# Mamba-2 scan into a SwiGLU layer: mean of squares by four 32-column tiles, the roots spread by a load, and a new order of steps

## The chip, the cores and the metric

The kernel runs on one core of a Trainium2 chip. The core has five engines that run side by side, each through its own list of instructions in order: TensorE (PE; its weight loads are shown apart as PEld), VectorE (DVE), ScalarE (ACT), GpSimd (POOL) and SyncE (SP). SP here only issues transfers (DMAs), which 16 DMA engines carry out; ACT issues four at the start. Matrix products read operands from SBUF and write into banks of PSUM, from where DVE or ACT take them. The metric is device time of one execution in microseconds.

## The reference, cut to what matters

```python
# part one: batch, heads, seq, head_dim, d_state = 4, 8, 768, 32, 16
log_a = np.log(np.clip(a, 1e-6, 1.0))
for c in range(nc):                       # chunks of 32 along seq
    cum = np.cumsum(la, axis=-1)
    L = np.exp(cum[:, :, :, None] - cum[:, :, None, :]) * causal
    y_intra = (einsum('bhin,bhjn->bhij', Cc, Bc) * L) @ xc
    y_inter = einsum('bhin,bhnd->bhid', Cc, state) * np.exp(cum)[..., None]
    y[:, :, sl] = y_intra + y_inter
    state = decay_full * state + sum over j of Bx * decay_from_j
# part two: 3072 tokens, d_model 256, d_ff 1536
rms = np.sqrt(np.mean(x * x, axis=-1, keepdims=True) + 1e-06)
xn = x / rms * rms_g
g = xn @ w_gate
val = xn @ w_val
out = (g / (1 + np.exp(-g)) * val) @ w_out
```

Everything is float32. `x` of part two is y with the heads side by side: one row of 256 values for each of 3072 tokens. `rms` is one number for each token; the change is about how it is computed and handed to the 128 partitions.

## The kernel before, in words

The 3072 tokens are worked in six blocks of 512, each made of two pairs of 256 tokens (pair = two chunks of 128, cut in halves of 64 from the third pair on). Activations lie transposed: a partition is a feature, a column a token. Part one gives, for a block, y in PSUM (the steps `turn`, `T`, `Tt`, `Td`: transposes of B and C and their copies; `g`, `gg`, `L`, `L1`: products and decays; `A`, `S`: state additions and states; `y`: outputs). Then, for each block:

- `sq` (L733 to L749): ACT squares y, POOL adds the two halves of the 256 features, so `sqs[blk]` is 128 partitions by 512 tokens. `yt` copies y to SBUF.
- `ms` (`norm_sums`, L772): one product on PE with the constant `mean` (128 x 128, all 1/256) as weights and `sqs[blk]` as the moving operand. All 128 output partitions hold the same 512 means.
- `rs` (`norm_roots`, L776 and L777): ACT takes Ln and then Exp with scale -0.5, which is one over the root, on 128 x 512 into `r`.
- `xn` (`norm_apply`, L784): DVE multiplies y, the gains and `r`, one half of the features at a time. Block 0 has another form (L788), and its first two weight products run ahead of the roots (`early`, `norm`).
- `tx` (L868): differences of the quarters of xn. Gate and value products then follow Winograd's form of Strassen's scheme: seven products instead of eight, `P.k.j` for k of 1 to 7 and j of 0 to 5 (L891). `take` (L897) copies a bank to SBUF on ACT, `C` (L903) adds on DVE, `silu` (L912) runs on ACT, `hid` (L916) multiplies on DVE. Block 0 uses plain products (`gate`, L807) for its first six columns of weights and `P` for the others.
- `O.k.j` (L981) is the projection to the output by the same scheme; block 0 has the plain `o` (L923). `Otake`, `Oadd` and `out` end it.

Weights come in eight-byte words and are cut down to float32 while the first block runs: `fetch` loads a piece (k of 0 to 19), `pow` (ACT, L182 to L185), `man` and `wt` (DVE, L192 to L201) convert it; `cw` and `two` make sums of weights. `bc.p` and `x.p` load B, C and x of a pair, `rowout` and `rowe` store rows of decays to DRAM, and `dT` and `spread` load them back spread over partitions (L530, L461). `bank` takes a PSUM bank out of two that these steps share.

The order of work is written out by hand: the string `order` names some 1,540 steps, `block:step.numbers/slot`, and they are issued in exactly this order. Each engine, and SP as the queue of transfers, executes its part of that list in order, and semaphores hold an instruction until what it reads is there and what it overwrites is read. From block 1 on, a step written under block n that belongs to part one or to the norm (`ms`, `rs`, `xn`, `y` and others) works for block n+1; `1:ms` is for block 2. Tiles of one tag share buffers: `r` has the tag `sq2` (one buffer), row tiles have `r_sb` (three). A step that needs exponentials after a SiLU, or the other way, makes ACT load a table; `table` and `exps` load one ahead of need.

Of the kernel before, what the change touches and what calls it, by code (L numbers as in the profile page):

```python
# [9 lines left out]
FP32 = mybir.dt.float32  # L10
# [10 lines left out]
def kernel(  # L21
# [35 lines left out]
    P = 128  # L57
# [709 lines left out]
    xns = {}  # L767

    def norm_sums(blk):

        ps["m", blk] = ms = bank("ms", (P, TB))
        nc.tensor.matmul(out=ms, lhsT=mean, rhs=sqs[blk], start=True, stop=True)  # L772

    def norm_roots(blk):
        ps["r", blk] = r = nrm.tile([P, TB], FP32, tag="sq2", name="r", bufs=1)
        nc.scalar.activation(out=r, in_=ps.pop(("m", blk)), func=AF.Ln, bias=eps)  # L776
        nc.scalar.activation(out=r, in_=r, func=AF.Exp, scale=-0.5)  # L777

# [312 lines left out]
    def by_vector(out, in_, scale):  # L1091
# [25 lines left out]
        "ms": norm_sums, "rs": norm_roots, "xn": norm_apply,  # L1117
# [27 lines left out]
    def of_chunk(n, fn):  # L1145
# [19 lines left out]
        "ms": when(1, norm_sums), "rs": when(1, norm_roots), "xn": when(1, norm_apply),  # L1165
# [7 lines left out]
        0:warm 0:a 0:set 0:bc.0 0:bc.1 0:x.0 0:x.1 0:ident 0:fetch.0 0:ones 0:zeros 0:fetch.1 0:upto  # L1173
        0:gcol 0:never 0:after 0:fetch.2 0:mid 0:ident16 0:whole16 0:fetch.3 0:idle.7 0:mask.0.0/1
        0:mask.0.1/0 0:hmask 0:part 0:part2 0:fetch.4 0:head 0:mids 0:fetch.5 0:bc.2 0:x.2 0:fetch.6
        0:aT 0:la0 0:log4.0.4 0:fetch.7 0:log 0:fetch.9 0:mask.1.1/2 0:log4.4.2 0:log4.6.2 0:sel
        0:upto2 0:after2 0:whole 0:r.0 0:tmask 0:fetch.15 0:parts.0 0:middles 0:c*2 0:turn.0.1
        0:T.0.1 0:cx 0:kinks 0:eps 0:Tt.0.0.1 0:d 0:dx 0:Tt.0.1.1 0:sums.0.1 0:exp.0.1 0:turn.0.0
        0:Tt.0.0.0 0:T.0.0 0:Tt.0.1.0 0:scale.1 0:cc 0:sums.0.0 0:exp.0.0 0:scale.0 0:mean
        0:turn.1.0 0:never16 0:g.0.1/0 0:L.0.1 0:man.0 0:turn.1.1 0:T.1.1 0:Tt.1.1.0 0:Tt.1.1.1  # L1180
        0:Tt.1.0.0 0:T.1.0 0:Tt.1.0.1 0:sums.1.1 0:exp.1.1 0:g.0.0/1 0:L.0.0 0:bc.4 0:man.1 0:pow.0
        0:last.0 0:Tl.0 0:A.0 0:S.0 0:pow.1 0:mask.1.0/0 0:sums.1.0 0:exp.1.0 0:wt.0 0:g.1.1/2
        0:L.1.1 0:pow.5 0:row.1 0:rowout.1 0:rowe.1 0:wt.1 0:g.1.0/1 0:L.1.0 0:man.5 0:fetch.8
        0:last.1 0:Tl.1 0:man.2 0:y.0/0 0:mask.3/2 0:A.1 0:S.1 0:wt.5 0:r.1 0:y.1/1 0:sq.0 0:yt.0
# [185 lines left out]
```

## Time and profile before

| | |
|---|---|
| time, three runs | 408.11, 407.00, 405.97 us; median 407.0 |
| the profiled execution | 407.43 us, of which the span of instructions is 405.7 |
| granted PE clock in it | 0.999 of full |
| busy: PE, DVE, ACT, POOL | 398.3, 300.1, 220.9, 36.6 us |
| matmul passes | 3851 |
| DMA | 25.35 MB, mean 62 GB/s |
| ACT table loads | 16, 1283 ns each |

Times of the profile count from the start of the span. A line of the timeline gives start, length, engine, line of the kernel, operation, what is written from what, the shape and how many instructions were merged; in brackets the engine's idle time before them and what ended it. `128*32` is the part of the PE array that a pass uses, rows by columns. A float32 matmul appears as two passes. Matmuls overlap in a pipeline and their ends are modelled, so a group's cost is read from its start to the start of the next one. A PE that counts as busy can still be waiting inside.

### The profile page before, as it was taken

To read this page: it belongs to the slowest core of one execution; us is meant where nothing else is said; L and a number is where in the kernel's file an instruction comes from. 1 tells how busy PE (TensorE), PEld (TensorE's weight loads), DVE (VectorE), ACT (ScalarE), POOL (GpSimd) and SP (SyncE) were. 2 spreads that over 40 slices of the span, in tenths; PEclk is the share of its full clock that TensorE was granted. 3 is DMA by queue.
4 is the path that set the end of the run, shared out by engine and by line. 5 is a ranking of instruction groups with operands and counts; after the bars stand their busy time and mean duration, and the time that the engine had idled before them with its cause. 6 is when DMAs were issued, how large, how long until landed. Compare 5 with 4: busy or idle time off the path is not lost.

```text
span 405.7 us, 9479 instructions
## 1 busy us (share of the span) xinstructions
PE 398.3 (98%) x3851; PEld 340.1 (84%) x3851; DVE 300.1 (74%) x686; ACT 220.9 (54%) x451; POOL 36.6 (9%) x57
## 2 busy tenths in 40 slices
PE   8999999999999999999999999999999999999997
PEld 4556467888888899888899988899988899988896
DVE  5998999979877878468799348788358676266682
ACT  3899796975756334655554545360754462544500
POOL 4010010002300011300023000010500010000000
PEclk9999999999999999999999999999999999999999
DMA  9897997800001041550350000330100000100001
GB/s 112 229 253 165 216 227 129 175 18 0 2 1 53 11 135 42 66 75 29 82 93 2 13 0 2 90 109 2 52 2 0 2 4 0 53 0 2 0 2 53
DMA packets 88995, 25.35 MB, mean 62 GB/s; under 512 B 76888, under 2 KB 82776, under 8 KB 88952
## 3 DMA queue, kind: packets, MB, share of 16 engines
q1 hardware_dynamic: 84792, 24.49, 27.8%
q10 hardware_dynamic: 4160, 0.26, 0.7%
q8 instruction: 30, 0.49, 0.5%
q14 instruction: 13, 0.11, 0.1%
HBM read 21.33 MB, written 3.41 MB: 61 GB/s over the span
## 4 chain that ended last, share of the span: by engine, by line
PE 84%; SPq 4%; DVE 4%; DMA 4%; ACT 2%; issue 1%; ACTq 0%; DVEq 0%
PE gate L891 28%; PE o L981 23%; PE val L891 21%; PE o L923 5%; PE y L699 3%; SPq L121 2%; SPq L128 1%; PE g L562 1%; DMA wr<-in_moe_w_gate_dram 1%; DMA dT<-rowe 1%; PE ms L772 1%; PE tp L505 1%; DMA br<-in_B_dram 1%; SPq L160 1%; DVE h L840 1%; DMA rowe<-e_sb 1%
## 5 line engine op out<-in xcount | busy, mean ns | idle before, releaser
L903 DVE TENSOR_TENSOR c<-val,p 128x512 f32<-128x512 f32 x99 | 67.4, 687 | 40.8 <-PE val L891 32.6
L897 ACT COPY p<-gate 128x512 f32<-128x512 f32 x99 | 57.5, 584 | 55.9 <-PE gate L891 54.3
L891 PE MATMUL gate<-tx,sw 128*128 128x256 f32 x264 | 66.1, 381 | 0.0
L912 ACT ACTIVATE c<-c 128x256 f32<-128x256 f32 x99 | 39.6, 417 | 41.6 <-DVE c L903 41.4
L891 PEld LDWEIGHTS gate<-tx,sw 128*128 128x128 f32 x264 | 49.3, 190 | 7.8 <-ACT p L897 1.0
L916 DVE TENSOR_TENSOR h<-c 128x256 f32<-128x256 f32 x99 | 40.1, 418 | 16.1 <-ACT c L912 16.0
L891 PE MATMUL val<-xn,sw 128*128 128x256 f32 x132 | 33.7, 380 | 0.0
L891 PE MATMUL val<-tx,sw 128*128 128x256 f32 x132 | 33.6, 381 | 0.0
L891 PE MATMUL gate<-xn,wgv 128*128 128x256 f32 x132 | 33.4, 383 | 0.0
L891 PE MATMUL val<-xn,wgv 128*128 128x256 f32 x132 | 33.4, 379 | 0.0
L891 PE MATMUL gate<-tx,wgv 128*128 128x256 f32 x132 | 33.2, 380 | 0.0
L475 POOL TENSOR_SCALAR_AFFINE_SELECT L<-L 64x512 f32<-64x512 f32 x32 | 23.0, 719 | 79.1 <-ACT L L473 77.6
L981 PE MATMUL o<-wo,h 128*128 128x128 f32 x240 | 30.1, 276 | 0.0
L981 PEld LDWEIGHTS o<-wo,h 128*128 128x128 f32 x240 | 28.9, 192 | 1.4 <-issue 0.7
L981 PE MATMUL o<-two,h 128*128 128x128 f32 x240 | 29.1, 275 | 0.0
L981 PEld LDWEIGHTS o<-two,h 128*128 128x128 f32 x240 | 28.2, 192 | 1.0 <-issue 0.7
L981 PE MATMUL o<-two,s 128*128 128x128 f32 x240 | 28.7, 275 | 0.0
L997 ACT COPY v<-o 128x256 f32<-128x256 f32 x15 | 5.7, 377 | 41.9 <-PE o L981 41.9
L981 PEld LDWEIGHTS o<-two,s 128*128 128x128 f32 x240 | 27.8, 192 | 0.1
L891 PEld LDWEIGHTS val<-tx,sw 128*128 128x128 f32 x132 | 24.8, 190 | 3.5 <-issue 0.2
L891 PEld LDWEIGHTS gate<-tx,wgv 128*128 128x128 f32 x132 | 24.8, 190 | 3.4
L891 PEld LDWEIGHTS val<-xn,sw 128*128 128x128 f32 x132 | 24.8, 190 | 3.3
(184 smaller groups left out, 636.5 us busy)
## 6 DMA issues: line engine op xcount, KB each, us to landing
L<-rowd SPq DMA_DIRECT2D x32, 128.0 KB, 3.5
xr<-in_x_dram SPq DMA_DIRECT2D x24, 128.0 KB, 3.1
wr<-in_moe_w_out_dram SPq DMA_DIRECT2D x6, 512.0 KB, 6.1
wr<-in_moe_w_gate_dram SPq DMA_DIRECT2D x5, 512.0 KB, 4.5
wr<-in_moe_w_val_dram SPq DMA_DIRECT2D x5, 512.0 KB, 7.3
out_dram<-ob SPq DMA_DIRECT2D x9, 256.0 KB, 2.4
br<-in_B_dram SPq DMA_DIRECT2D x22, 64.0 KB, 4.0
cr<-in_C_dram SPq DMA_DIRECT2D x22, 64.0 KB, 2.6
```

The lines of the kernel that those rows point to most:

```text
L121: queues[i].dma_start(out=dst[:, i], in_=src[b, :, sl, :].rearrange("h s n -> s h n"))
L128: queue.dma_start(out=st[p]["x"][:, i], in_=x[b, :, sl, :].rearrange("h s n -> s h n"))
L475: nc.gpsimd.affine_select(out=L[r], in_=L[r], pattern=[[0, NH], [1, HC]], compare_op=ALU.is_ge, fill=0.0, base=0, channel_multiplier=-1)
L699: nc.tensor.matmul(out=y[2 * k + u][rows, (2 * n + i) * HC:(2 * n + i + 1) * HC], start=(k, u, rows.start) not in opened, stop=True, skip_ ...
L891: nc.tensor.matmul(out=dst[:, half[w]], lhsT=lhsT, rhs=rhs, start=(k in (1, 2, 5) and w == 0), stop=True, skip_group_check=True)
L897: nc.scalar.copy(out=t, in_=Xs[j])
L903: nc.vector.tensor_tensor(out=t, in0=Zs[j], in1=a, op=ALU.add)
L912: nc.scalar.activation(out=u, in_=src[:, half[0]], func=AF.Silu)
L916: nc.vector.tensor_tensor(out=hidden_tile(blk, j)[:, c // 10 - 1, c % 10 - 1], in0=u, in1=src[:, half[1]], op=ALU.mult)
L923: nc.tensor.matmul(out=o, lhsT=hs_[blk, f // 2][:, f % 2, k // 2, (k % 2) * P:(k % 2 + 1) * P], rhs=wo[:, f], start=opens, stop=(f == NF - ...
L981: nc.tensor.matmul(out=o[t] if apart else o[:, t * P:(t + 1) * P], lhsT=lhsT[:, t], rhs=rhs, start=(k in (1, 2, 4, 5) and j == 0 and (apar ...
L997: nc.scalar.copy(out=ts[k], in_=halves_of(Os["X"]))
```

## The change

For blocks 1 to 5 the one `ms` product is replaced by four: `mean` is cut to 32 columns, and each product takes 128 of the 512 tokens and writes 32 partitions of a 128 x 128 result (`tile_position` names the 32 columns of the array). Partition 32k+q then holds token 128k+m in column m, 32 times over. Ln and Exp run on 128 x 128. The result is stored to DRAM (`roots`, 64 KB), and a new step `rb` (`spread_roots`) loads one of the 32 equal rows of each group back into all 128 partitions (256 KB into `r`); `xn` is as before. Block 0 keeps its form. The first 12 steps of the order, through `0:fetch.1`, stay; the later ones stand in a new order, with the five `rb` among them. Of the order the diff shows both versions up to block 0's last gate products, and the places around `rs`, `rb` and `xn`.

```diff
--- before.py
+++ after.py
@@ -764,17 +764,35 @@
                  in_=y.rearrange("p u (j m) -> p u j m", j=n))
 
 
-    xns = {}
+    xns, roots = {}, {}
 
     def norm_sums(blk):
 
-        ps["m", blk] = ms = bank("ms", (P, TB))
-        nc.tensor.matmul(out=ms, lhsT=mean, rhs=sqs[blk], start=True, stop=True)
+        if blk == 0:
+            ps["m", blk] = ms = bank("ms", (P, TB))
+            nc.tensor.matmul(out=ms, lhsT=mean, rhs=sqs[blk], start=True, stop=True)
+            return
+        ps["m", blk] = ms = bank("ms", (P, P))
+        for k in range(NT):
+            nc.tensor.matmul(out=ms[32 * k:32 * k + 32], lhsT=mean[:, 0:32],
+                             rhs=sqs[blk][:, k * P:(k + 1) * P], start=True, stop=True,
+                             tile_position=(0, 32 * k), skip_group_check=True)
 
     def norm_roots(blk):
-        ps["r", blk] = r = nrm.tile([P, TB], FP32, tag="sq2", name="r", bufs=1)
+        if blk == 0:
+            ps["r", blk] = r = nrm.tile([P, TB], FP32, tag="sq2", name="r", bufs=1)
+        else:
+            r = nrm.tile([P, P], FP32, tag="r_sb", name="r4", bufs=3)
         nc.scalar.activation(out=r, in_=ps.pop(("m", blk)), func=AF.Ln, bias=eps)
         nc.scalar.activation(out=r, in_=r, func=AF.Exp, scale=-0.5)
+        if blk:
+            roots[blk] = dram.tile([NT, 32, P], FP32, name="roots%d" % blk)
+            nc.sync.dma_start(out=roots[blk].rearrange("t q m -> (t q) m"), in_=r)
+
+    def spread_roots(blk):
+        ps["r", blk] = r = nrm.tile([P, TB], FP32, tag="sq2", name="r", bufs=1)
+        nc.sync.dma_start(out=r.rearrange("p (t m) -> p t m", t=NT),
+                          in_=roots[blk][:, 0].partition_broadcast(P))
 
     def norm_apply(blk):
         r = ps["r", blk]
@@ -1114,7 +1132,7 @@
         "yt": lambda p: taken_out(p, ac.copy),
         "ydone": lambda p: leave(("y", p)),
         "pow": power, "man": mantissa, "wt": weight,
-        "ms": norm_sums, "rs": norm_roots, "xn": norm_apply,
+        "ms": norm_sums, "rs": norm_roots, "rb": spread_roots, "xn": norm_apply,
         "early": lambda f, s: products_early(
             f, s, take("gate", ("gv", f)) if s == 0 else ps["gv", f]),
         "norm": lambda f: (normed(f), leave(("gv", f))),
@@ -1162,7 +1180,8 @@
         "y": of_pair(1, lambda p: outputs(p, pair_of_banks("y", 2) if p % 2 == 0 else None,
                                           [p + 2] if p + 2 < NPAIR else [], p % 2)),
         "sq": when(1, lambda b: squares(2 * b)), "yt": when(1, lambda b: taken_out(2 * b, ac.copy)),
-        "ms": when(1, norm_sums), "rs": when(1, norm_roots), "xn": when(1, norm_apply),
+        "ms": when(1, norm_sums), "rs": when(1, norm_roots),
+        "rb": when(1, spread_roots), "xn": when(1, norm_apply),
         "tx": when(1, combine_x),
         "bc": of_pair(2, load), "x": of_pair(2, load_x), "spread": of_chunk(2, spread), "sub": of_chunk(2, subtract),
         "ex": of_chunk(2, exponential), "scale2": of_pair(2, scale),
@@ -1170,160 +1189,160 @@
         "exps": when(1, lambda b: ac.preload_act_table_set("natural_log_exp_and_others")),
     }
     order = """
-        0:warm 0:a 0:set 0:bc.0 0:bc.1 0:x.0 0:x.1 0:ident 0:fetch.0 0:ones 0:zeros 0:fetch.1 0:upto
-        0:gcol 0:never 0:after 0:fetch.2 0:mid 0:ident16 0:whole16 0:fetch.3 0:idle.7 0:mask.0.0/1
-        0:mask.0.1/0 0:hmask 0:part 0:part2 0:fetch.4 0:head 0:mids 0:fetch.5 0:bc.2 0:x.2 0:fetch.6
-        0:aT 0:la0 0:log4.0.4 0:fetch.7 0:log 0:fetch.9 0:mask.1.1/2 0:log4.4.2 0:log4.6.2 0:sel
-        0:upto2 0:after2 0:whole 0:r.0 0:tmask 0:fetch.15 0:parts.0 0:middles 0:c*2 0:turn.0.1
-        0:T.0.1 0:cx 0:kinks 0:eps 0:Tt.0.0.1 0:d 0:dx 0:Tt.0.1.1 0:sums.0.1 0:exp.0.1 0:turn.0.0
-        0:Tt.0.0.0 0:T.0.0 0:Tt.0.1.0 0:scale.1 0:cc 0:sums.0.0 0:exp.0.0 0:scale.0 0:mean
-        0:turn.1.0 0:never16 0:g.0.1/0 0:L.0.1 0:man.0 0:turn.1.1 0:T.1.1 0:Tt.1.1.0 0:Tt.1.1.1
-        0:Tt.1.0.0 0:T.1.0 0:Tt.1.0.1 0:sums.1.1 0:exp.1.1 0:g.0.0/1 0:L.0.0 0:bc.4 0:man.1 0:pow.0
-        0:last.0 0:Tl.0 0:A.0 0:S.0 0:pow.1 0:mask.1.0/0 0:sums.1.0 0:exp.1.0 0:wt.0 0:g.1.1/2
-        0:L.1.1 0:pow.5 0:row.1 0:rowout.1 0:rowe.1 0:wt.1 0:g.1.0/1 0:L.1.0 0:man.5 0:fetch.8
-        0:last.1 0:Tl.1 0:man.2 0:y.0/0 0:mask.3/2 0:A.1 0:S.1 0:wt.5 0:r.1 0:y.1/1 0:sq.0 0:yt.0
-        0:ydone.0 0:early.0.0/0 0:row.0 0:scale.2 0:pow.3 0:parts.1 0:sums.3 0:man.6 0:pow.2 0:wt.2
-        0:sq.1 0:ms.0 0:yt.1 0:ydone.1 0:early.0.1 0:pow.6 0:fetch.11 0:wt.6 0:rowe.0 0:dT.2 0:man.3
-        0:exp.3 0:rs.0 0:pow.4 0:mask.2/1 0:sums.2 0:exp.2 0:man.7 0:bc.3 0:turn.2 0:T.2 0:wt.3
-        0:early.1.0/2 0:early.1.1 0:Tt.2.1 0:x.4 0:x.3 0:xn.0 0:rowout.0 0:man.4 0:wt.4 0:gate.2/1
-        0:fetch.10 0:norm.0 0:norm.1 0:man.8 0:Tt.2.0 0:Td.2 0:gg.2/0 1:table 0:silu.0 0:hid.0
-        0:pow.7 0:wt.7 0:L1.2.3 0:man.9 0:L.2.0 0:L1.2.2 0:pow.9 0:wt.9 0:silu.2 0:hid.2 0:tx.0
-        0:pow.8 0:wt.8 0:dT.3 0:gate.3/2 0:silu.3 0:hid.3 0:fetch.12 0:pow.11 0:scale.3 0:man.10
-        0:fetch.13 0:A.2 0:S.2 0:gate.4/0 0:silu.4 0:hid.4 0:bc.5 0:fetch.14 0:man.11 0:fetch.16
-        0:cw.3 0:pow.10 0:gate.5/1 0:silu.5 0:hid.5 0:pow.12 0:y.2/2 0:S.3 0:yt.2 0:sq.2 0:ydone.2
...
-        0:o.9 0:hidg.21.5 0:rs.1 0:xn.1 1:P.1.0 1:P.1.1 1:P.2.1 1:P.2.0 0:tx.1 0:ex.11 1:x.0
...
-        1:O.6.5 1:s4.4 1:Otake.6 1:s4.3 2:spread.2 1:spread.3 2:turn.0 2:T.0 2:Tt.0.1 2:Tt.0.0 1:ms
-        1:rs 1:O.7.0 1:O.7.1 1:O.7.2 1:O.7.3 1:O.7.4 1:O.7.5 1:Otake.7 1:O.2.5 1:spread.2 1:sub.2
-        1:sub.0 1:ex.0 1:O.4.5 1:xn 2:P.1.1 2:take.1.1 1:Oadd.22 1:O.3.0 1:O.3.1 1:O.3.2 1:Oadd.11
...
-        2:O.6.3 2:O.6.4 2:O.6.5 2:s4.2 2:s4.1 2:s4.3 1:out.1 2:s4.4 2:rs 3:turn.1 2:xn 2:tx 2:O.2.3
...
-        3:s.5 3:s3.5 3:exps 2:out.1 3:ms 3:rs 3:s.4 3:s3.4 3:O.1.0 3:O.1.1 3:O.1.2 3:O.1.3 3:O.1.4
...
-        4:O.6.3 4:sq 4:ms 4:rs 4:xn 4:s4.2 4:O.2.2 4:O.6.4 4:O.6.5 4:s4.5 4:Otake.6 4:s4.4 4:O.4.1
...
+        0:warm 0:a 0:set 0:bc.0 0:bc.1 0:x.0 0:x.1 0:ident 0:fetch.0 0:ones 0:zeros 0:fetch.1 0:mean
+        0:head 0:upto 0:never 0:after 0:mid 0:upto2 0:gcol 0:mids 0:ident16 0:whole16 0:idle.7
+        0:mask.0.0/1 0:whole 0:hmask 0:tmask 0:part 0:part2 0:sel 0:mask.1.1/0 0:fetch.5 0:after2
+        0:aT 0:la0 0:kinks 0:mask.0.1/2 0:log4.0.4 0:r.0 0:parts.0 0:eps 0:log 0:d 0:dx 0:c*2 0:cx
+        0:log4.4.2 0:log4.6.2 0:scale.0 0:bc.2 0:turn.0.1 0:T.0.1 0:Tt.0.0.1 0:Tt.0.1.1 0:sums.0.1
+        0:exp.0.1 0:turn.0.0 0:Tt.0.1.0 0:T.0.0 0:Tt.0.0.0 0:sums.0.0 0:exp.0.0 0:fetch.2 0:turn.1.1
+        0:T.1.1 0:Tt.1.0.1 0:Tt.1.1.1 0:scale.1 0:cc 0:g.0.1/2 0:L.0.1 0:turn.1.0 0:Tt.1.1.0
+        0:Tt.1.0.0 0:T.1.0 0:sums.1.1 0:exp.1.1 0:A.0 0:S.0 0:A.1 0:S.1 0:man.0 0:g.0.0/1 0:L.0.0
+        0:pow.0 0:wt.0 0:man.5 0:pow.1 0:never16 0:last.1 0:Tl.1 0:mask.1.0/2 0:sums.1.0 0:exp.1.0
+        0:g.1.0/0 0:L.1.0 0:scale.2 0:last.0 0:Tl.0 0:fetch.4 0:fetch.3 0:x.4 0:middles 0:man.1
+        0:g.1.1/1 0:L.1.1 0:fetch.6 0:fetch.7 0:pow.5 0:wt.5 0:y.0/2 0:sq.0 0:pow.3 0:row.1
+        0:rowout.1 0:rowe.1 0:yt.0 0:ydone.0 0:fetch.12 0:y.1/0 0:r.1 0:row.0 0:man.2 0:fetch.9
+        0:fetch.8 0:wt.1 0:early.0.0/1 0:parts.1 0:man.6 0:mask.3/2 0:sums.3 0:pow.2 0:wt.2 0:rowe.0
+        0:rowout.0 0:dT.2 1:dT.0 0:sq.1 0:ms.0 0:yt.1 0:ydone.1 0:early.0.1 0:pow.6 0:wt.6
+        0:fetch.13 0:man.3 0:exp.3 0:rs.0 0:man.7 0:wt.3 0:turn.2 0:pow.4 0:xn.0 0:mask.2/0 0:sums.2
+        0:exp.2 0:early.1.0/2 0:early.1.1 0:man.4 0:wt.4 0:gate.2/0 0:x.2 0:norm.0 0:norm.1 0:T.2
+        0:Tt.2.0 0:Tt.2.1 0:Td.2 0:dT.3 0:gg.2/1 1:table 0:silu.0 0:hid.0 0:gate.3/2 0:tx.0 0:man.8
+        0:pow.7 0:wt.7 0:L1.2.3 0:L1.2.2 0:man.9 0:silu.2 0:hid.2 0:L.2.0 0:pow.9 0:wt.9 0:A.2 0:S.2
+        0:pow.8 0:wt.8 0:silu.3 0:hid.3 0:fetch.11 0:man.11 0:pow.11 0:gate.4/0 0:silu.4 0:hid.4
+        0:bc.3 0:scale.3 0:fetch.10 0:pow.10 0:man.10 0:cw.3 0:gate.5/1 0:silu.5 0:hid.5 0:x.3
...
+        0:rs.1 1:turn.0 0:hidg.11.4 0:hidg.21.4 0:hidg.22.4 1:T.0 1:Tt.0.0 0:silug.21.5 0:hidg.12.4
+        0:P.3.5 0:C.12.5 0:man.19 0:pow.19 0:wt.19 0:hidg.21.5 0:silug.12.5 0:hidg.12.5 0:spread.11
+        0:sub.11 0:ex.11 0:table.0 0:sub.8 0:o.6 0:o.7 0:o.8 0:o.9 0:o.10 1:T.1 1:Tt.1.0 0:rb.1
+        0:xn.1 1:P.1.1 1:take.1.1 1:P.1.0 1:take.1.0 1:P.2.1 1:P.2.0 0:tx.1 1:P.6.1 1:take.6.1
...
+        1:s2.2 1:O.5.3 1:O.5.4 1:s2.4 1:s2.3 1:O.5.5 1:s2.5 1:s3.2 1:s3.0 1:sub.2 1:ms 1:rs 1:O.6.0
+        1:s4.0 1:O.6.1 1:O.6.2 1:s4.1 1:O.6.3 1:O.6.4 1:O.6.5 1:Otake.6 1:s4.3 1:s4.4 2:turn.0 2:T.0
+        2:Tt.0.1 1:rb 1:s4.5 1:s4.2 1:s3.5 2:dT.1 2:turn.1 2:T.1 2:Tt.1.0 2:Tt.1.1 2:Tt.0.0 2:Td.0
...
+        2:scale2.1 1:O.4.3 1:O.4.4 1:O.4.5 1:Oadd.21 1:O.2.3 1:O.2.4 1:O.2.5 1:O.3.0 1:O.3.1 1:xn
+        2:P.1.1 2:take.1.1 2:P.1.0 2:take.1.0 1:tx 1:ex.2 1:spread.1 1:sub.1 1:ex.1 1:O.3.2 1:O.3.3
...
+        2:P.4.5 2:silu.21.5 2:spread.3 2:sub.3 2:P.3.4 2:C.12.4 2:spread.1 2:exps 2:P.3.5 2:ms 2:rs
+        2:silu.12.4 2:hid.21.5 2:s.1 2:hid.22.5 2:C.12.5 2:O.2.0 2:O.2.1 3:turn.1 3:T.1 3:Tt.1.1
+        3:Tt.1.0 2:s.2 2:s3.2 2:hid.22.4 2:hid.11.4 2:hid.12.4 2:hid.21.4 2:s.4 3:spread.0
+        2:silu.12.5 2:hid.12.5 2:s3.4 3:turn.0 2:rb 2:s3.3 2:s3.1 1:out.0 2:s.5 2:s3.5 2:O.5.0
...
+        4:dT.0 3:ms 3:O.1.0 3:O.1.1 3:O.1.2 3:O.1.3 3:O.1.4 3:rs 3:rb 3:O.1.5 3:Otake.1 3:O.5.0
...
+        4:hid.12.4 4:O.2.1 4:O.2.2 4:O.2.3 4:O.2.4 4:exps 4:O.1.4 4:ms 4:rs 4:hid.22.5 4:O.2.5 4:s.5
...
+        4:rb 4:xn 5:P.1.1 5:take.1.1 3:out.1 4:Oadd.22 4:O.3.0 4:Oadd.11 4:Oadd.21 5:P.1.0
...
```

## The prediction

> **What bounds the kernel now.** I read four views in this order: the page's first two parts, the stages (busy time in chosen stretches), the chain that ended last, and the timelines of PE and DVE in the stages that matter. The page, then the stages:
>
> ```profile
> span 405.7 us, 9479 instructions
> PE 398.3 (98%) x3851; PEld 340.1 (84%) x3851; DVE 300.1 (74%) x686; ACT 220.9 (54%) x451; POOL 36.6 (9%) x57
> ...
> PE 84%; SPq 4%; DVE 4%; DMA 4%; ACT 2%; issue 1%; ACTq 0%; DVEq 0%
> ```
>
> ```profile
> 20.00:30.00 10.00, 9.02 (x160) 5.67 (x151) 9.72 (x23) 9.48 (x19) 1.46 (x2) 1.00 1.00 258
> 70.00:80.00 10.00, 10.00 (x50) 8.65 (x49) 9.86 (x21) 9.14 (x16) 0.00 (x0) 1.00 0.88 185
> 80.00:90.00 10.00, 10.00 (x48) 8.81 (x47) 7.48 (x16) 6.93 (x13) 0.00 (x0) 1.00 0.18 26
> 150.00:160.00 10.00, 10.00 (x86) 9.52 (x85) 8.42 (x18) 4.41 (x12) 1.45 (x1) 1.00 0.25 74
> ```
>
> The columns are the stretch, its length, then busy time of PE, PEld, DVE, ACT, POOL, the granted clock, the DMA share and GB/s. There are two stages. Up to about 75 us VectorE has 9.1 to 9.9 of every 10 us; PE looks busy, but its passes are few and wait inside. From 75 us on PE is full and the chain is PE alone: there PE time saved is time saved, while ACT (54%) and DVE have room. The granted clock is 1.00 throughout, so it explains nothing here.
>
> The PE timeline gives what a step costs (start, time, passes; an f32 matmul is two passes):
>
> ```profile
> 19.75 1.08 PE L677 MATMUL y<-L,xr 128*32 128x128 f32 x32 [0.21 <-ACT L L455]
> 20.76 0.45 PE L668 MATMUL y<-T,S 32*64 32x128 f32 x8
> ...
> 129.67 1.03 PE L891 MATMUL val<-xn,wgv 128*128 128x256 f32 x4
> 130.63 1.21 PE L562 MATMUL g<-T 32*64 32x128 f32 x64
> 131.77 1.13 PE L891 MATMUL val<-tx,sw 128*128 128x256 f32 x4
> ...
> 155.37 0.38 PE L505 MATMUL tp<-ident,cr 128*128 128x128 f32 x2
> 155.59 1.02 PE L772 MATMUL ms<-sq,mean 128*128 128x512 f32 x2
> ```
>
> A start less the next start is what a group occupies; recorded lengths overlap. The mean-of-squares product starts at 155.59 and the next group at 156.45: 0.86 us, the same in all blocks. A product group (two matmuls) occupies 0.864 us.
>
> The DVE timeline shows its large waits in the first stage:
>
> ```profile
> 2.88 0.37 DVE L273 TENSOR_REDUCE head<-ident 128x8 f32<-128x128 f32 x1
> 5.30 0.36 DVE L307 TENSOR_SCALAR early<-aT 128x192 f32<-128x192 f32 x1 [2.05 <-PE aT L303]
> ...
> 34.27 0.29 DVE L1062 COPY r_sb<-r_ps 128x128 f32<-128x128 f32 x1 [0.53 <-DMA rowd<-r_sb]
> ...
> 40.57 0.42 DVE L536 TENSOR_TENSOR T<-tp,dT 128x256 f32<-128x256 f32 x1 [0.70 <-ACT e L182]
> ```
>
> The last wait is ended by the load of dT (40.48 us, the chain says), not by ACT. It holds PE too: g resumes at 41.14 after 0.52 us, and the third gate product starts at 41.72. From there to the end are 364.0 us, and by such rows PE has 361 of work: 231 products (199.6), 210 `O` at 0.446 (93.7), twelve `o` at 1.73 (20.7), three gate products (10.4), and 37 of tiled steps, turns, `ms` and changes between them. So whatever the start loses or gains before that product reaches the end.
>
> **The change, part by part.**
>
> *Mean of squares on PE.* Five of six `ms` steps (blocks 1 to 5) lose 0.86 us each, 4.30 in all. Each gets four tiles of 32 columns with 128 moving columns, eight passes. The trace has that very shape: L677, 32 passes from 19.75 to 20.76, 31.6 ns each, so 0.25 us. Changing between tiled and whole-array work costs: a product occupies 0.864 us, yet 0.96 lie between 129.67 and the tiled g, and 0.96 again between 131.77 and 132.73. That is 0.10 us each way, 0.20 per `ms`, and the new order leaves all five between whole-array steps. New cost 0.45, saved 0.41, times five: 2.05 us, all on the path. Bounds: 3.05 saved if no change is paid, and 1.0 lost if the tiles don't overlap (eight passes at the 0.109 us of the 128-column transposes are 0.87, plus 0.20). I take 2.05, since both rows are of exactly this kind.
>
> The Trainium skill, TensorEngine Tiling (Array Packing), "Theoretical Speedup", offers up to 4x for such tiles; an estimate by it is 0.22 us for a step and 3.2 us saved. Its "Key Properties" speak against that: changing the tiling mode drains the array. The 0.10 us rows show this drain, and no figure of the page is needed.
>
> *The roots on ACT.* Ln and Exp over 512 columns (688 and 630 ns) become 128 columns; the nearest rows are 257 ns (L1069) and 308 ns (L312), together 0.57 instead of 1.32, so 3.7 us less in five blocks. The new order needs 21 table loads for 16, five times 1283 ns, 6.4 us more. Net 2.7 us more on ACT, costed at nothing: ACT is idle 46% of the span. If that cover is gone, 2.7 us. Block 4 has two of these loads between its own Ln and Exp, so they count in the next item.
>
> *The round trip of the roots.* Before, the apply step followed Exp at once. Now SP issues a 64 KB store and, when it has landed, a 256 KB load, five times; ten issues more on SP. Chain from Ln to the first half of xn: 0.57, store 1.8 (the 128 KB output rows; upper bound 2.94, the rowe store in the loaded start), load 3.4 (the 128 KB L spreads; upper bound 5.8, their slowest), first half of xn 0.75, hand-overs about 0.3. That is 6.8 us, at most 10.4. The cover is PE work that the new order puts between the `rs` step and the first product of the next block: block 1 has five `o` at 1.73, one product at 0.86 and one turn at 0.44, 9.9 us; block 2 has 21 `O` at 0.446 and two turns, 10.3; then 17.0, 13.0 and 11.6 by the same count. Every cover exceeds the chain, block 4's by 3.6 even with two table loads (9.4 of 13.0). Before, the covers were 0, 3.6, 4.9, 14.3 and 7.6, so the order was made over for this. Cost nothing; upper bound 0.6 (0.5 and 0.1 in blocks 1 and 2). Behind the waiting load SP has L spreads, dT and x loads of the next blocks, due many steps later; behind the waiting xn DVE has `tx` and hidden units of the same block, which PE cannot use sooner. The POOL queue changes no work. In blocks 1 and 3 two L spreads (1.2 us of issue) go between store and load and run while the store lands.
>
> The Trainium skill, DMA: Bandwidth & Descriptors, "Anatomy of one DMA", gives a fixed 2.0 us and bytes over 436 GB/s, for another issuing path. As an estimate that is 2.15 and 2.6, 4.75 for both legs where the rows give 5.2; the chain would be 6.4 and hidden as well. [...]
>
> *The new order in the first stage.* DVE executes the same 686 instructions, 334.5 us by mean rows. Summed up to a landmark, before and after: weight 4 34.4 and 34.4; second normed 37.1 and 37.1; Td.2 38.7 and 37.5; fourth hidden 47.4 and 48.8; S.3 56.3 and 56.3; weight 14 74.8 and 74.8. The amount of work ahead is the same; only waits can go. Ahead of the 5.30 us instruction DVE now has 4.25 us instead of 2.88: 1.37 us of small constants fall into the 2.05 us wait. For dT, rowe's second store now comes ahead of the second square and the 8 us that the loads of B and C (bc.4, 23.7 to 31.7) hold SP fall behind; so the 0.70 wait should go, and the 0.53 one likewise. What is late next is DVE itself. Taken: 1.4 us, the constants alone, since I cannot time the transfers behind the other two waits. Bounds: 2.6 gained (all three), and 0.8 lost if the moved fetches (5 ahead of 2 to 4, 12 ahead of 8 and 9, x.2 late) make waits like the two that transfers ended before (0.53 and 0.25). By the page's 112, 229 and 253 GB/s the first fetched 512 KB is in at about 14 us and first used at about 17.
>
> *The order from 75 us.* By the same count the smallest PE distance between two products in one bank is as large as before (0.86 once, then 1.3), and few are under 1.7 us (three, was eight); the copy between them takes 584 ns. Up to xn of block 1 DVE has 100.0 us of work instead of 95.8, 4.2 more; against it stand 2.5 us that xn waited in PE's queue (94.66 to 97.15), 2.5 us idle in 80 to 90 and one more `o` (1.73) ahead. Cost nothing, cover 2.5 us left.
>
> **Sum.** 2.05 + 1.4 = 3.45 us less. The profiled execution took 407.43, so 404.0; it stands 0.4 above the median of 407.0, against which I give **403.6**.
>
> **Rivals.** (a) *Only PE's part arrives*: the first stage is held by transfers or ACT instead, nothing of 1.4 us comes: 405.0. For it: DMA is at 1.00 in 20 to 30 us. Against: DVE's 9.7 beside it. (b) *The tiles do not overlap*, so the change doesn't do what it says: 407.0 + 1.0 - 1.4 = 406.6. Against: L677. (c) *Slower: the round trip outlasts its cover.* With a chain of 12.1 us PE stands 2.2, 1.8, 1.7 (block 4 with its loads) and 0.5 us before the blocks, 6.2 in all: 409.8; at 13 us it is 413. The gain is eaten from about 11.4 us on. For it: SP is one queue, and the same kind of chain, rowe to dT, took 32.41 to 40.48 in the loaded start. Against: after 75 us the DMA share is mostly under 0.6. (d) *All bounds are met*: 3.05 + 2.6, 401.4.
>
> **How the numbers follow.** The forecast has 0.50, (d) 0.12, (a) 0.12, (b) 0.05, (c) with unforeseen stalls of the new order 0.21. About 0.5% (2 us) is what a measurement of this kernel tells from no change, so faster means under 405.0: forecast and (d), 0.62; same 0.17; slower 0.21. The forecast's own range is 402 to 405. To hold 8 in 10 it goes from 401.0, under (d), to 409.5, near the start of (c).
>
> **What would show it.** Right: `ms` rows of 128*32 with 40 passes, about 0.45 us between neighbours; PE full from 75 us on; the 2.05 us wait of DVE down to about 0.7; the third gate product at 40.3 or sooner; loads of r landing under 6 us after the store's issue. Wrong: PE idle before the first product of blocks 1 or 2, ended by DVE xn; ms groups of 1 us; a new DMA wait on DVE before 40 us.

## The result, and the profile after

The changed kernel takes 406.13 us (median of 20 runs, 405.33 to 407.69); the kernel before, beside it, 407.06 us (20 runs, 405.95 to 408.83). The ratio is 0.9976, with a 95% interval of 0.9964 to 0.9988: 0.9 to 1.0 us faster, where I forecast 3.45. The time lies inside the range of 401.0 to 409.5, but outside the forecast's own 402 to 405, and within 0.5% of no change, to which I had given 0.17. The profiled execution took 406.08, with a span of 404.3.

The first parts of its page, as shown of before:

```profile
span 404.3 us, 9559 instructions
PE 395.5 (98%) x3881; PEld 338.6 (84%) x3881; DVE 296.5 (73%) x686; ACT 223.9 (55%) x456; POOL 37.6 (9%) x57
...
PE 85%; DVE 6%; DMA 4%; ACT 2%; issue 1%; SPq 1%; DVEq 0%; ACTq 0%
```

PE is busy for 2.8 us less, but the span is only 1.4 shorter: PE stands 1.4 us longer. Two of the stages shown of before and one more (stretch, length, busy time of PE, PEld, DVE, ACT and POOL, granted clock, DMA share, GB/s) say where:

```profile
20.00:30.00 10.00, 8.67 (x114) 5.45 (x111) 9.72 (x23) 8.60 (x17) 1.50 (x2) 1.00 0.91 250
...
150.00:160.00 10.00, 9.54 (x86) 9.35 (x84) 5.40 (x15) 3.37 (x9) 1.43 (x2) 1.00 0.43 74
160.00:170.00 10.00, 9.18 (x50) 8.35 (x51) 6.78 (x13) 6.25 (x12) 4.26 (x6) 1.00 0.91 105
```

In the kernel before, the last of these was:

```profile
160.00:170.00 10.00, 10.00 (x60) 9.15 (x59) 6.11 (x13) 6.04 (x11) 5.57 (x8) 1.00 0.25 43
```

From 150 to 170 us PE, full in the kernel before, lacks 1.28 us. The chain that ended last, cut to that place (start, length, what), names the cause:

```profile
148.74 0.40 PE ms L777 x8
149.14 0.02 issue
149.16 0.38 ACT r L786
149.54 0.02 issue
149.56 0.32 ACT r L787
149.88 0.02 issue
149.90 1.54 DMA roots<-r
...
151.52 8.38 DMA r<-roots
159.90 0.02 issue
159.92 0.76 DVE xn L802
160.69 0.14 issue
160.82 1.96 PE gate L909 x8
```

Roots (0.72 with the hand-over between them), store (1.54) and the half of xn (0.76) are near what I took. The load of the roots takes 8.4 us; I had taken 3.4 and at most 5.8. From Ln to the end of the first half of xn are 11.5 us, and the cover of block 2 was 10.3. PE's list of waits from 66 us on (engine, line, for whom: us, times, longest) shows 1.3 us behind xn; the wait for the sum c at 65 us comes up again below:

```profile
PE gate L909 <- DVE xn L802: 1.3, 1, 1.3
PE val L909 <- DVE c L921: 0.8, 1, 0.8
...
```

So the theory to test: *the round trip gave 1.5 us back, and it is slow because all 512 packets of its load, 512 bytes each, read one place in memory*. "One place" or "one row" stands here for the first of the 32 equal rows: in the changed kernel four pieces of 512 bytes, 16 KB apart, each read by 128 packets; where the roots are stored row by row, one piece of 2 KB. Rivals: the new order itself loses the time; or the load is slow for its shape, its number of packets or the traffic beside it.

### The profile page after: what moved, and what is told of

Read it like the earlier page. It is cut to its first block, busy times and chain, and to the rows that moved or that the text cites. A ratio compares the mean times of both kernels' runs of the same rounds, so it can differ in the third digit from the quotient of the medians.

```text
span 404.3 us, 9559 instructions
## 1 busy us (share of the span) xinstructions
PE 395.5 (98%) x3881; PEld 338.6 (84%) x3881; DVE 296.5 (73%) x686; ACT 223.9 (55%) x456; POOL 37.6 (9%) x57
## 4 chain that ended last, share of the span: by engine, by line
PE 85%; DVE 6%; DMA 4%; ACT 2%; issue 1%; SPq 1%; DVEq 0%; ACTq 0%
PE gate L909 28%; PE val L909 21%; PE o L999 17%; PE o L941 5%; PE gate L825 3%; PE y L699 3%; DMA r<-roots 2%; DMA dT<-rowe 2%; PE gate L835 1%; PE g L562 1%; PE y L627 1%; PE e L426 1%; DVE m L195 1%; DVE wgv L201 1%; DVE xn L802 1%
## 5 line engine op out<-in xcount | busy, mean ns | idle before, releaser
L915 ACT COPY p<-gate 128x512 f32<-128x512 f32 x99 | 57.4, 581 | 51.9 <-PE gate L909 47.6
L934 DVE TENSOR_TENSOR h<-c 128x256 f32<-128x256 f32 x99 | 40.4, 420 | 11.4 <-ACT c L930 10.9
L909 PEld LDWEIGHTS gate<-xn,wgv 128*128 128x128 f32 x132 | 24.3, 190 | 5.3 <-issue 1.6
```

The lines of the kernel that those rows point to most:

```text
L909: nc.tensor.matmul(out=dst[:, half[w]], lhsT=lhsT, rhs=rhs, start=(k in (1, 2, 5) and w == 0), stop=True, skip_group_check=True)
L915: nc.scalar.copy(out=t, in_=Xs[j])
L934: nc.vector.tensor_tensor(out=hidden_tile(blk, j)[:, c // 10 - 1, c % 10 - 1], in0=u, in1=src[:, half[1]], op=ALU.mult)
```

## The experiments

Median and ratio are against the kernel before on the same chip, whose median moved between 407.3 and 408.3 from job to job; ratios are what can be compared.

### The order alone, and the change without its round trip

The first is the order of the changed kernel, which differs from the 13th step on, with the old norm:

```diff
     def norm_sums(blk):
-        if blk == 0:
-            ps["m", blk] = ms = bank("ms", (P, TB))
-            nc.tensor.matmul(out=ms, lhsT=mean, rhs=sqs[blk], start=True, stop=True)
-            return
-        ps["m", blk] = ms = bank("ms", (P, P))
-        for k in range(NT):
...
+        ps["m", blk] = ms = bank("ms", (P, TB))
+        nc.tensor.matmul(out=ms, lhsT=mean, rhs=sqs[blk], start=True, stop=True)
...
     def spread_roots(blk):
-        ps["r", blk] = r = nrm.tile([P, TB], FP32, tag="sq2", name="r", bufs=1)
...
+        pass
```

> The new order of all steps from the 26th, with the old norm (one 512-column product with the mean, roots on 128x512, no trip through memory; the step that spreads the roots does nothing). Theory (the round trip gave the gain back): the changed kernel loses some 1.5 us of TensorE's time to it (TensorE idle 1.44 us between 150 and 225 us of the changed kernel's profile, none there before), so the order alone is worth what the first stage gained: changed kernel 406.1 plus five steps at 0.43 us more (+2.15), less 1.5 = 406.8 us, ratio to before 0.999. Rival (the order itself is the loser after 75 us, the trip costs nothing): 406.1 + 2.15 = 408.3 us, ratio 1.003, and TensorE idles behind the same steps of blocks 2 and 3 as in the changed kernel.

The second keeps the tiles and leaves the store and the load out, so that each partition multiplies by the roots of its own tile for all four:

```diff
-            roots[blk] = dram.tile([NT, 32, P], FP32, name="roots%d" % blk)
-            nc.sync.dma_start(out=roots[blk].rearrange("t q m -> (t q) m"), in_=r)
+            ps["r", blk] = r
...
-                                               scalar=gcol[:, t:t + 1], in1=r,
+                                               scalar=gcol[:, t:t + 1],
+                                               in1=r.unsqueeze(1).to_broadcast([P, NT, P]),
```

> The changed kernel without the round trip: VectorE multiplies by the 128x128 roots as they lie in SBUF, repeated for each of the four column tiles, so the spreading of the roots is left out (each partition uses the roots of its own tile for all four tiles). It prices the trip by leaving it out. Theory: the trip costs 1.5 us: 404.6 us, ratio 0.994, TensorE full from 150 to 225 us, and the landing of the L spreads and of the x, B and C loads back at 3 to 4 us. Rival (the trip is hidden, the order loses): 406.1 us as the changed kernel, TensorE idle in the same places.

Measured: the order alone 407.09 us, ratio 0.998 (0.9963 to 0.9996); without the trip 405.16, ratio 0.9939 (0.9917 to 0.9961). Stages of 75 us, first of the order alone, then without the trip, then of the changed kernel (columns as above):

```profile
150.00:225.00 75.00, 75.00 (x754) 68.33 (x753) 54.58 (x123) 37.35 (x78) 8.94 (x11) 1.00 0.25 53
```

```profile
150.00:225.00 75.00, 75.00 (x764) 68.41 (x763) 53.74 (x121) 36.56 (x78) 8.96 (x12) 1.00 0.25 52
```

```profile
150.00:225.00 75.00, 73.56 (x748) 66.51 (x747) 52.90 (x120) 35.35 (x75) 8.89 (x11) 1.00 0.33 61
```

The new order loses nothing from 75 us on: PE is full in both. The differences of the ratios give the parts: order 0.0020 (0.8 us), tiles 0.998 - 0.9939 = 0.0041 (1.7 us), round trip 0.9976 - 0.9939 = 0.0037 (1.5 us lost). The intervals of the three ratios are ±0.5 to ±0.9 us wide, so that a part that is a difference of two is known to about ±1 us; the idle 1.44 us of PE, absent in both others, says the last one more sharply.

### One place or many

Two loads that read all 32 equal rows of the roots in place of one. The first also stores the roots row by row, so that a packet has 2 KB:

```diff
-            nc.sync.dma_start(out=roots[blk].rearrange("t q m -> (t q) m"), in_=r)
+            nc.sync.dma_start(out=roots[blk].rearrange("q t m -> t q m"), in_=r)
...
-        nc.sync.dma_start(out=r.rearrange("p (t m) -> p t m", t=NT),
-                          in_=roots[blk][:, 0].partition_broadcast(P))
+        nc.sync.dma_start(
+            out=r, in_=roots[blk].rearrange("q t m -> q (t m)").unsqueeze(0).to_broadcast([NT, 32, TB]))
```

> The changed kernel with the roots stored row by row (32 equal rows of 2 KB) and the load reading row p mod 32 into partition p: 128 packets of 2 KB from 32 places in memory instead of 512 packets of 512 bytes from one place of 2 KB. Theory (the load takes 8 us because all its packets read one place: some 40 packets of 512 bytes start in each 0.5 us of it, 42 GB/s, at 34 ns each, so 13 of 16 engines stand idle): landing falls from 8 us to 3 to 4 us, the waits of xn for r go, 404.7 us, ratio 0.994. Rival (the engines are slow for another reason, the queue or the bytes): landing stays over 6 us and the time at 406.1.

The second keeps the 512 packets of 512 bytes:

```diff
+        for k in range(NT):
+            nc.sync.dma_start(
+                out=r[32 * k:32 * k + 32].rearrange("p (t m) -> p t m", t=NT),
+                in_=roots[blk].rearrange("t q m -> q t m"))
```

> As the changed kernel (512 packets of 512 bytes), but four loads of 32 partitions each, and partition 32k+q reads the equal row q: so the packets stay as they are and only the place they read is spread over 32 rows. If the one place is the cause, the loads land in 3 to 4 us after the first's issue although there are 512 packets, and the time is 404.7 us, a little more for three issues of 0.36 us each on SP. If the number or the size of the packets is the cause, they land after 8 us as before and the time stays at 406.1 us or above.

Measured: 0.9947 (0.9926 to 0.9967) with 2 KB, and xn waits for r as long as in the changed kernel (5.9 us, three times), which was not expected; 0.9934 (0.9906 to 0.9961) with 512 bytes, and no wait at all. The first ratio is not explained: in its profile PE stands 1.3 us behind xn as in the changed kernel, and its runs spread from 404.4 to 408.0 us. The rates tell the three loads apart. GB/s from 330 to 345 us in 40 slices, where block 5's load is alone on the queues but for two output stores (the 300s are those stores); the changed kernel, then the four loads of 512 bytes, then the 2 KB load:

```profile
GB/s 0 0 0 0 0 0 0 0 0 143 103 347 279 25 37 45 44 45 44 31 38 44 46 41 46 52 79 82 89 146 184 193 101 55 0 0 0 0 0 0
```

```profile
GB/s 0 0 0 0 0 0 0 0 5 169 210 350 139 76 126 139 142 156 254 358 148 0 0 0 0 0 0 0 0 44 0 0 0 0 0 0 0 0 0 0
```

```profile
GB/s 0 0 0 0 0 0 0 0 0 0 0 23 120 332 322 98 0 0 0 153 279 120 104 87 109 27 98 109 87 96 98 74 0 0 0 0 0 0 0 0
```

44 GB/s for some 4 us in the changed kernel, 126 to 156 in the second, which is about the pace of its issues (four loads of 64 KB in 1.74 us of SP), so that 32 rows may allow more. The packet records show the third: four packets at a time, 84 ns each, one behind the other. So two causes stood: the place, and the shape of a load.

The next two take the place back to one row, by four loads for 32 partitions each, and by four for one column tile each; the third stores the roots row by row and has one load of 128 packets of 2 KB from one row.

```diff
+        for k in range(NT):
+            nc.sync.dma_start(
+                out=r[32 * k:32 * k + 32].rearrange("p (t m) -> p t m", t=NT),
+                in_=roots[blk][:, 0].partition_broadcast(32))
...
+        for k in range(NT):
+            nc.sync.dma_start(out=r[:, k * P:(k + 1) * P], in_=roots[blk][k, 0].partition_broadcast(P))
...
+        nc.sync.dma_start(
+            out=r, in_=roots[blk][0].rearrange("t m -> (t m)").partition_broadcast(P))
```

> The four loads of 32 partitions of the run before, but all read the one row 0, as the changed kernel does: against that run only the place differs. The run with 2 KB packets from 32 rows landed late although the places differed (its packets ran four at a time, 84 ns each, one behind the other), so two causes stand: place (packets that read one place are served one in 12 ns, which is the pace of the changed kernel's load, 512 packets in 6.2 us) and shape (one load with an outer or middle dimension of four runs on some four engines, and the four loads ran side by side). Place: the loads land some 8 us after the first issue, 406.1 us, ratio 0.9976. Shape: they land in 2 us as before, xn does not wait, ratio 0.9934 to 0.995.

> Four loads, each for all 128 partitions and one column tile of 512 bytes, from one place: 512 packets of 512 bytes as in the changed kernel, no dimension of four. Place: 512 packets at 12 ns, lands 8 us after the first issue, ratio 0.9976. Shape: lands within 3 us of the last issue, ratio 0.9935 to 0.995.

> One load in which all 128 partitions read one row of 2 KB (roots stored row by row): one place, one load, 128 packets, no dimension of four. Shape: the load spreads over all engines, 128 packets of 84 ns on 16 of them = 0.7 us and some 2 us around, lands in 3 us, ratio 0.9935 to 0.995. Place, if it counts by packets at 12 ns: 1.6 us and 2 us around, the same; if it counts by bytes (42 GB/s): 6.2 us, lands at 8, ratio 0.9976.

Measured: 0.9989 (0.9967 to 1.0011), 0.9993 (0.9972 to 1.0014) and 0.9927 (0.99 to 0.9954). The lists of loads (number, KB each, median us from a load's own issue to its landing), of the changed kernel, of the four loads from one row, of the four by column tile, and of the 2 KB row:

```profile
r<-roots SPq DMA_DIRECT2D x5, 256.0 KB, 8.2
```

```profile
r<-roots SPq DMA_DIRECT2D x20, 64.0 KB, 7.0
```

```profile
r<-roots SPq DMA_DIRECT2D x20, 64.0 KB, 7.4
```

```profile
r<-roots SPq DMA_DIRECT2D x5, 256.0 KB, 3.2
```

Four loads instead of one change nothing while they read one row: xn waits 5.4 and 6.0 us for r. With the same bytes in a quarter of the packets, the load lands in 3.2 us. In the packet records some 44 packets start in each 0.5 us of the loads from one row, 11.4 ns apart, whether of 512 bytes or, at the peak, of 2 KB: the pace goes by number, not by bytes.

Half the packets (two of the four column tiles) test this by dose:

```diff
-        nc.sync.dma_start(out=r.rearrange("p (t m) -> p t m", t=NT),
-                          in_=roots[blk][:, 0].partition_broadcast(P))
+        nc.sync.dma_start(out=r[:, 0:256].rearrange("p (t m) -> p t m", t=2),
+                          in_=roots[blk][0:2, 0].partition_broadcast(P))
```

> The changed kernel with a load of two of the four column tiles only: 256 packets of 512 bytes from one place; VectorE uses them for both halves of the columns, so the roots of two tiles are left out. If packets of one place come one per 11.5 ns (44 in each 0.5 us of the changed kernel's load, whether of 512 bytes or of 2 KB), landing falls from 8.2 us to 8.2 - 256 * 0.0115 = 5.3 us and xn's waits for r from 5.7 us to under 1; if the 8.2 us are a fixed delay of this load, it lands at 8 us again.

And 128 packets of 2 KB from four rows, with the roots stored row by row and an outer dimension of 32, test the shape:

```diff
+            out=r, in_=roots[blk][0:4].rearrange("q t m -> q (t m)").unsqueeze(0).to_broadcast([32, NT, TB]))
```

> One load of 128 packets of 2 KB, partition p reading row p mod 4: the outer dimension of its source is 32, the inner one four. The load from 32 rows, outer dimension four, ran its packets four at a time, 84 ns each. If the outer dimension sets how many engines serve a load, this one runs on all of them, 128 packets of 84 ns on 16 engines = 0.7 us, and lands in 2.5 to 3.2 us, the time as with one row, 404 us; if another thing slowed that load, such as the rows' number or the store row by row, it lands after 5 us as there.

The same lists, half the packets and then four rows:

```profile
L<-rowd SPq DMA_DIRECT2D x32, 128.0 KB, 5.2
...
r<-roots SPq DMA_DIRECT2D x5, 128.0 KB, 5.3
```

```profile
L<-rowd SPq DMA_DIRECT2D x32, 128.0 KB, 3.5
...
r<-roots SPq DMA_DIRECT2D x5, 256.0 KB, 3.5
```

5.3 us as worked out beforehand, and xn waits no more. The four rows land in 3.5, and some 16 of their packets run at once where the load with the outer dimension four ran four: there it was the shape. The Trainium skill, DMA: Bandwidth & Descriptors, section "Why a DMA increments its semaphore by 16 and not by 1", says that a transfer uses the largest number of engines, up to 16, that divides the slowest dimension of both its patterns; the runs agree, about 4 packets at once with 4 and about 16 with 32. The same page's "Specifications" give 512 bytes as the least transfer for the line rate; here the size alone settled nothing: packets of 512 bytes moved 126 to 156 GB/s from 32 rows and 44 from one.

The times of these two, one run each, are 406.86 and 405.86; by single runs of this kernel nothing under 0.5% can be told.

### The old order with the new norm

The order of before, with `rb` put directly behind `rs` in all five blocks (against the kernel before; two of the five places):

```diff
-        0:o.9 0:hidg.21.5 0:rs.1 0:xn.1 1:P.1.0 1:P.1.1 1:P.2.1 1:P.2.0 0:tx.1 0:ex.11 1:x.0
+        0:o.9 0:hidg.21.5 0:rs.1 0:rb.1 0:xn.1 1:P.1.0 1:P.1.1 1:P.2.1 1:P.2.0 0:tx.1 0:ex.11 1:x.0
...
-        1:rs 1:O.7.0 1:O.7.1 1:O.7.2 1:O.7.3 1:O.7.4 1:O.7.5 1:Otake.7 1:O.2.5 1:spread.2 1:sub.2
+        1:rs 1:rb 1:O.7.0 1:O.7.1 1:O.7.2 1:O.7.3 1:O.7.4 1:O.7.5 1:Otake.7 1:O.2.5 1:spread.2 1:sub.2
```

> The order of before with the new norm, the load directly behind the store: what the trip costs where the order does not cover it. Products between the roots and the first product of the next block in the old order, by the program: 0, 3.6, 4.9, 14.3 and 7.6 us for blocks 1 to 5. Chain from the sums to the first product: 0.7 (roots) + 1.5 (store) + 8 (load) + 0.75 (xn) + 0.5 of hand-overs = 11.5 us. TensorE idles 11.5 + 7.9 + 6.6 + 0 + 3.9 = 30 us, less 1.9 saved in the sums: 435 us, ratio 1.07. If the trip were as cheap as I took it (6.8 us): 6.8 + 3.2 + 1.9 = 12 us, less 1.9: 417 us, ratio 1.025.

Measured: 444.38 us, ratio 1.0915 (1.0874 to 1.0956), 9 us more than worked out. PE's waits, then VectorE's for r and for L:

```profile
PE gate L909 <- DVE xn L802: 22.0, 4, 10.8
PE o L999 <- DVE ob L1026: 4.6, 2, 2.7
```

```profile
DVE xn L802 <- DMA r<-roots: 26.6, 4, 11.0
...
DVE L L467 <- DMA L<-rowd: 12.9, 1, 12.9
```

PE stands before blocks 1, 2, 3 and 5, for 6.0, 10.8, 1.7 and 3.5 us, where I had worked out 11.5, 7.9, 6.6 and 3.9; before block 4 it does not, as worked out. In blocks 1 and 3 ACT ran ahead with the roots: their stores are issued at 92.72 and 235.26, 5 and 9 us before PE runs out of work. In block 2 it is longer because of what queues behind the load: two L spreads are issued behind it (169.11, the load 168.68), and the subtraction that needs them stands ahead of xn on VectorE and waits 12.9 us for them. In the other four blocks xn waits for r itself, the 26.6 us.

That makes 22.0 us behind xn, 8 less than worked out, and yet the time is 9 us more. PE also waits 4.6 us for ob, output sums of VectorE, and two lines of this run's page show the rest:

```profile
PE 409.5 (92%) x3881; PEld 348.1 (79%) x3881; DVE 297.7 (67%) x686; ACT 218.2 (49%) x451; POOL 36.1 (8%) x57
...
PEclk9999999996999998699999899999999999599999
```

PE is busy for 14.0 us more than in the changed kernel with the same 3881 passes. The second line is the granted clock in 40 slices of 11 us, in tenths. By finer stretches it is 1.0 but for 102.7 to 109.4, 174.4 to 184.5, 249.5 to 252.7 and 375.8 to 385.9 us, where it is 0.50; each of the four begins 4 to 5 us after PE ran out of work. PE is busy for 20.4 us of them, which at the full clock would be about half: some 10 us (an estimate). In the other runs the clock is 0.996 or more, and in the changed kernel, where PE stands 1.3 us, it stays at 1.0. So the new order is what makes the trip bearable, some 38 us of it; by itself it gives the 0.8 us above.

### The load made short, and one step moved

The kernel with the one 2 KB row, again with more runs, and the same with block 0's sum c ahead of the last states on VectorE:

```diff
-        0:wt.12 0:pow.13 1:dT.1 0:fetch.18 1:S.0 1:S.1 0:sq.3 0:yt.3 0:ydone.3 0:C.22.3 0:silug.22.3
+        0:wt.12 0:pow.13 1:dT.1 0:fetch.18 1:S.0 0:C.22.3 1:S.1 0:sq.3 0:yt.3 0:ydone.3 0:silug.22.3
```

> The kernel whose load reads one row of 2 KB, once more and with more rounds beside the run above, since only four of its runs counted. Theory (the round trip is hidden when its load is 128 packets): my forecast's 403.6 us of a before of 407.0, ratio 0.992; rival (the few runs flattered it): 0.995 and over.

> The kernel whose load reads one row of 2 KB, with one step moved: block 0's sum C.22.3 on VectorE goes ahead of the last states (S.1) instead of behind them. In every profile of the new order TensorE waits there 0.76 us for VectorE's sum c (65 us). If that wait is what the first stage's gain was lost to, 0.6 to 0.8 us: ratio to before 0.9927 - 0.0017 = 0.991, and TensorE has no wait for c; if the wait only moves to a later product (VectorE's states are then late), the ratio stays at 0.9927 and another wait stands in the list.

Measured: 405.47 us, ratio 0.992 (0.9896 to 0.9944), and 404.09 us, ratio 0.9897 (0.9862 to 0.9932), beside a before of 408.27. PE's waits from 60 us on, first of the one and then of the other:

```profile
PE val L909 <- DVE c L921: 0.8, 1, 0.8
PE y L699 <- DVE L L601: 0.4, 1, 0.4
```

```profile
PE y L699 <- DVE L L601: 0.4, 1, 0.4
PE ms L777 <- issue: 0.3, 1, 0.3
```

The wait for c is gone and no other of its size stands in its place. The two intervals overlap, so that the move is worth 0.8 us is likely and not shown. Both kernels leave nothing out, and both intervals lie below no change.

## Why the prediction was right and wrong

*Mean of squares on PE: the way right, the saving a quarter too large.* The block 2 sums on PE's timeline, of the changed kernel and then of the order alone (start, length, group):

```profile
145.90 2.84 PE L999 MATMUL o<-two,s 128*128 128x128 f32 x24
148.67 0.43 PE L777 MATMUL ms<-sq,mean 128*32 128x128 f32 x8
149.03 2.94 PE L999 MATMUL o<-two,s 128*128 128x128 f32 x24
151.81 0.38 PE L505 MATMUL tp<-ident,br 128*128 128x128 f32 x2
```

```profile
146.51 2.84 PE L984 MATMUL o<-two,s 128*128 128x128 f32 x24
149.19 1.02 PE L772 MATMUL ms<-sq,mean 128*128 128x512 f32 x2
150.05 2.84 PE L984 MATMUL o<-two,s 128*128 128x128 f32 x24
152.73 0.38 PE L505 MATMUL tp<-ident,br 128*128 128x128 f32 x2
```

The tiles occupy 0.36 us instead of 0.86, the 24 passes ahead 2.77 instead of 2.68, and the 24 behind 2.78 instead of 2.68. So the two changes of tiling cost 0.09 and 0.10, as taken, but the eight passes 0.36, where I had taken 0.25 from 32 passes in a row. From the first of these groups to the transposes it is 5.91 us instead of 6.22: a step costs 0.55 us, forecast 0.45, and saves 0.31, forecast 0.41. The other four blocks save 0.30 or 0.31 as well, 1.5 us in all instead of 2.05; the two runs' ratios say 1.7. The speed of up to four times in the Trainium skill (TensorEngine Tiling (Array Packing), "Theoretical Speedup"), by estimate 0.22 us a step, was not reached. Rival (b) falls too, though its 406.6 us lay nearest to the time.

*The roots on ACT: right.* 0.68 us (367 and 310 ns) where I took 0.57; ACT is busy 3.0 us more, by 2.7 worked out, and the extra costs nothing: without the trip PE is full.

*The round trip: wrong, and this is the step that failed.* It was costed at nothing, at most 0.6. "load 3.4 (the 128 KB L spreads; upper bound 5.8, their slowest)" took the duration of a row that fits in kind, a broadcast, and in half the bytes, but not in packets: an L spread has 64 of 2 KB, this load 512 of 512 bytes, all from one place. At 11.4 ns a packet the 448 more are 5.1 us, and 3.4 + 5.1 is 8.5, near the 8.2 measured; the row itself would have given this, had I read its packets: in the kernel before, the 256 packets of four L spreads in a row (from 197.4 us) start 13 ns apart. The upper bound fell with the value, since it came from the same row. The estimate by the Trainium skill (DMA: Bandwidth & Descriptors, "Anatomy of one DMA"), 2.6 us for this load and for another issuing path, goes by bytes alone and fails in the same way: 8.2 us from one row, and 3.2 for the same bytes in 128 packets. With 11.5 us for the chain PE stands before block 2, the 1.3 us of "PE idle before the first product of blocks 1 or 2, ended by DVE xn" that I had named as the sign. Rival (c) named the mechanism; by its covers a chain of 11.5 us would have cost 1.6, 1.2 and 1.1 us before blocks 1, 2 and 4, and of these block 2's alone came. The other covers were longer than I had counted: from Ln to the first product 13.1 us lie in block 1 (84.65 to 97.78, counted 9.9), since ACT had run ahead of PE with the roots, and 14.4 in block 4 (269.01 to 283.42, counted 13.0). That only 1.5 us were lost, with a load more than twice as long as taken, is thus in part luck.

The load also kept others waiting, which I had costed at nothing: the L spreads behind it land in 5.9 us (median), in 3.3 to 3.9 where it is short or gone, and 3.5 in the kernel before. Where four slow loads stand ahead they land in 3.3 and 3.4, but one of their issues then takes up to 4.3 and 4.6 us on SP, against 1.5 in the kernel before.

*The new order in the first stage: direction right, size and reason wrong.* The third gate product starts at 40.25 us, forecast 40.3 or sooner, from 41.72. But the constants did not do it. VectorE's large waits there:

```profile
5.30 0.36 DVE L307 TENSOR_SCALAR early<-aT 128x192 f32<-128x192 f32 x1 [1.03 <-PE aT L303]
...
6.81 0.42 DVE L362 CAST first<-r_ps 128x256 bf16<-128x256 f32 x1 [1.12 <-PE r_ps L355]
...
37.51 0.41 DVE L536 TENSOR_TENSOR T<-tp,dT 128x256 f32<-128x256 f32 x1
```

The 2.05 us wait became 1.03 and, right behind it, 1.12 for r_ps: the constants had been VectorE's work during that second wait. The waits for dT and rowd (1.23 us), which I had left out because I could not time their transfers, are gone instead, and that is most of the 1.47. Of the order alone 0.8 us arrived (0.2 to 1.5 by its interval). What takes the rest is not shown. PE's 0.76 us wait for c at 65 us stands in the changed kernel and not in before, but before has a wait of 0.6 for yt there that the new order lacks. And one profile of each kernel says little about this stage: the first copy of a product out of PSUM starts at 54.7 to 58.0 us in the twelve profiles of the new order (mean 56.0; 55.27 in the one that I compared), at 56.7 and 57.4 in the two of the old. VectorE's waits for fetched weights and for rowd come and go between these profiles (up to 1.0 and 1.1 us): the loss that I set at 0.8 for moved fetches shows in some executions.

*The order from 75 us: right.* PE is full from 75 to 375 us with the order alone.

*Sum.* 1.5 + 0.8 - 1.5 = 0.8, against 1.0 by the ratio (0.5 to 1.5) and 1.4 in the spans. Of the 2.5 us that are missing from the forecast's 3.45, the trip has 1.5, the first stage 0.6 and the sums 0.5, within the ±1 us to which the parts are known. Without the slow load the parts give 2.3 us, a ratio of 0.994. The kernel with the short load has 0.992 (0.9896 to 0.9944); that interval holds this and the forecast's 0.992 alike, so it does not show that the rest of the forecast was right.

## What to carry to other kernels

When a duration is borrowed from another transfer, compare packets (number, size, how many places they read, outer dimension) before bytes, and take the upper bound from the count, not from the same row's slowest case. A broadcast from DRAM should read one long row with few packets: here storing the roots row by row made the same 256 KB land in 3.2 instead of 8.2 us. Where a change reorders a stage held by transfers, one profile of each kernel is no measure of it.

## What the runs showed of the hardware that I had not expected

- Packets that read one place start 11.4 ns apart (some 44 in 0.5 us), at 512 bytes as at 2 KB: 512, 256 and 128 packets land in 8.2, 5.3 and 3.2 us. So do those from the four column tiles' rows, 16 KB apart, that the changed kernel reads; packets from 32 rows do not (126 to 156 GB/s at 512 bytes). Four rows of 2 KB stand between: in block 5 their 128 packets start 11.7 ns apart on average, but up to 67 in one half microsecond. Why, and where the line runs, was not tried.
- Splitting the load over four transfers does not help while they read one row (7.0 and 7.4 us).
- A load whose outer dimension is four runs four packets at a time, 84 ns per 2 KB, so for xn 2 KB packets from 32 rows were no faster than 512-byte packets from one (waits of 5.9 and 5.7 us).
- The change between whole-array and tiled matmuls cost 0.09 us ahead of the tiles and 0.10 behind them, and eight tiled passes 0.36 us, where 32 in a row took 1.01.
- In the old order, where PE stood for 3.5 to 10.8 us (before block 3 for 1.7 and 1.9), the granted clock fell to 0.50 for 3 to 10 us, from 4 to 5 us after PE ran out of work.
